# A new issue order for a fused attention and feed-forward kernel: five engine queues, copy engines and ring buffers

## The chip, the cores and the metric

The kernel runs on one core of one Trainium2 chip. The metric is device time in microseconds (us). The three runs of the kernel before took 398.63, 402.89 and 396.58 us; their median is 398.63.

A core has five engines with a queue of instructions each, which each works off in order: TensorE (PE in the profile, with its weight loads PEld), VectorE (DVE), ScalarE (ACT), GpSimd (POOL) and SyncE (SP, which here only issues DMAs). They wait for each other by semaphores.

## What is computed

Causal attention with a decay from forget gates, over 8 batches, 8 heads, 576 positions and head width 64; the heads are then joined and go through a bilinear feed-forward layer with 4608 tokens, width 512 and inner width 1536.

```python
scores = scale * np.matmul(q, k.transpose(0, 1, 3, 2))
cum = np.cumsum(np.log(np.clip(f, 0.0001, 1.0)), axis=-1)
decay = cum[:, :, :, None] - cum[:, :, None, :]
scores = np.where(causal, -1000000000.0, scores + decay)
attn = softmax(scores)                      # over the last axis
x = np.matmul(attn, v).transpose(0, 2, 1, 3).reshape(4608, 512)
out = ((x @ w_a) * (x @ w_b)) @ w_out
```

## The kernel before, in words

**Work items.** The function builds a list `ops` of 2353 numbered operations (class `Op`), each with an engine (or a choice of engines), a function that issues its instructions, and the operations on which it depends. Costs, priorities and due times that are noted at each operation came from a planner and play no part any more: the order in which the operations are issued is written out in the string `ORDER` (operation numbers, a range where they follow one another). Each engine executes its own operations in that order. The string `CHOICE` gives a letter (D, A or P for DVE, ACT or POOL) for each operation that several engines can do: casts, copies out of PSUM and, in batches 0 and 1, the normalisation of the attention weights. The string `SLOTS` gives, ring by ring, the buffer number of each tile in the order in which tiles are taken. `laid_out` (L1330) reads `ORDER` and `CHOICE`; `slot` and `turn` (L158, L161) read `SLOTS`.

**Attention.** The 64 heads are worked in 32 pairs `t`, four pairs to a batch. For each pair, PE computes scores for five blocks of 128 query rows, in three steps `qk t.0`, `qk t.2` and `qk t.3` (L529 to L605). For the pairs from 4 on, a fused DVE instruction adds the decay and finds the row minimum (L674); for batch 0 the decay is added by more matmuls, and DVE only finds the maximum (L646). ACT takes the exponential with its row sum (L701, L705), DVE the reciprocal (L713, L715), and POOL (in some cases of batches 0 and 1 ACT) normalises the weights (L726, L724) in two tiles, PA for query blocks 0 to 2 and PB for blocks 3 and 4. The weights are transposed: in batch 0, and for part A in batch 1, by PE (`ptr`, tile psP) with a copy out of PSUM (`pev`), everywhere else by a transposing DMA from SP (`tr`, L740) into PTA and PTB. PE then multiplies with v (`pv`, tiles pv and pvx, L769 and L784) and a copy (`ev`) puts the result into xT, which the feed-forward reads.

**Loads.** q, k and v of a batch come by DMA: q and k in two halves each (`ld`), f32 into a ring of three landing buffers n32 by SP, then cast to f16 by POOL (`ca`), transposed by PE (`pt`, tile psT) and copied to qT or kT (`pe`). Batch 0 and the v of batches 0 and 1 are cast by the DMA itself, which POOL issues (L334, L305). POOL also issues the eleven loads of the weights wa, wb and wout (L510). The cumulated decay rows come by DMA to the tile spread, 24 times, or are spread by PE (`bm`, tile scd) with a copy (`bc`) for pairs 4 to 7.

**Feed-forward.** It is cut into blocks of 256, 256, 256, 384, six times 512, and 384 tokens. For each slice of 128 to 256 of the inner width PE computes psa = x wa and psb = x wb; ACT copies psa to f16, and DVE multiplies it with psb into a tile ht (L1073). pso = h wout follows, with a copy (`ocopy`) and a store. psa, psb, pso, the transposes and the spread tiles share four PSUM buffers `ff`; scores and pvx share two double ones, `sc`.

**Interleaving.** Feed-forward blocks whose tokens are done are issued between the attention steps of later pairs. At the start, before any xT is there, PE is kept busy with 24 `wake` operations of four dummy matmuls (L82). The matmuls have modes: row (two tiles of 64 rows: scores and transposes of q and k), column (two tiles of 64 columns: pv) and full.

**Operations that are spoken of below.** 2: identity; 5 to 28: wakes; 46 and 47, 58: loads of k of batch 0 (first half in two parts, second half); 52 and 53, 62: the same of q; 48, 49, 54, 55, 59, 63: their transposes; 50: copy of the first k; 66 to 70: v loads of batch 0; 71 to 78: loads of wa, wa, wb, wb (first third of the width) and wa, wa, wb, wb (the rest); 82: scores 0.0; 262, 274, 267, 279: k and q loads of batch 1; 275, 280: casts of its second halves; 287: a fill of POOL; 500: first q load of batch 2; 1061, 1097, 1098, 1099: last scores, A and B transpose and pv of pair 19; 1465, 1501, 1503: the same (without B) of pair 27; from 1707 on: feed-forward.

Of the kernel before, what the change touches and what calls it, by code (L numbers as in the profile page):

```python
# [25 lines left out]
def kernel(  # L26
# [13 lines left out]
    B, H, S, D = q.shape  # L40
# [64 lines left out]
    def paddings():  # L105
# [36 lines left out]
        PA:03210213021302130213021302130213;PB:01101010101010101010101010101010;S:010110100110100110101011001101  # L142
        01010101001010101010101010010011010100101001000100010011011010011100111011010101110101;a16:0210210210210
        21021021021021021021201201210210210210201201201012012021021021020120120201010201210201201201201201021;bc
        :0210210210210210210210210210;ff:03120312032100023120310323231232301230103010103203013120312031203120312
        03123012310120213203203013203210312013201320130123021312312031232013012013023103210131310321320312031023
        10210321032130230231023102312302130213021321023023012032032031310210210312310231302132013203210310231023
        20120210102120321312012013203103021301321301302102302310230132031203120132013012012021023101301321032132
        030231031031032031230123201230312312312312312312302311021021302301231231230;ht:0dcba981234567d0bc9a18234
        5670dbc9a182543d670cb9a1428653d70cb2a9154863d7bac025914863dcb7a9205148dc36a9b72051483cdb6;n16:0110100101  # L150
        10001010010101010101;n32:0210201201201201020101212110210220201212202101;nv:01010101;osb:0101010101001010
        10101010010100110101;qd:010101010101010101010101;sc:0101010101010101010101011010010101100010101011001001
        0101101010101011010101010101010100101011101100101010110101100101100100101010;st:054321503421503421503421
        50342150
# [1054 lines left out]
    for n in cuts:  # L1209
# [3 lines left out]
        0 1 29 30 46 2 52 62 5 3 31 37 32 38 33-36 39 40 42 41 53 47 58 4 43 267 262 279 6-9 54 48 10 56  # L1213
# [27 lines left out]
        630 1792-1794 618 493 491 1795 492 494 631 702 707 653 654 703 697 1797 569 704 626 623 632 619  # L1241
# [4 lines left out]
        1827 1829-1831 709 719 723 767 671 681 591 729 628 724 647 636 682 655 648 641 1828 666 1832 686  # L1246
# [15 lines left out]
        1920 1914-1918 929 918 766 1919 951 970 975 1014 852 851 896 895 1871 919 1921 958 920 959 955  # L1262
# [111 lines left out]
```

## Time and profile before

| | |
|---|---|
| median of three runs | 398.63 us (396.58 to 402.89) |
| span of the profiled execution, from the first to the last instruction | 397.5 us (its own total time is not listed beside it) |
| PE busy | 386.4 us (97%), 5768 matmuls |
| DVE busy | 293.0 us (74%) |
| ACT busy | 290.6 us (73%) |
| POOL busy | 257.8 us (65%) |
| DMA | 76.87 MB, mean 193 GB/s |

A row of the timeline shows the start, the duration, the engine, the line, and the tiles written and read, with a count where instructions of one kind follow each other; in brackets stands the idle time ahead of it and what ended it. A row of the grouped view shows busy time, mean duration in ns, and idle time ahead by what ended it. A matmul's end is modelled and its 0.17 us or so of run-out overlaps the next one, so for PE the distance between starts says more than a duration. A row of the DMA issues shows kilobytes and the median time to landing.

### The profile page before, as it was taken

What the parts mean: (1) busy time and instruction counts of PE and PEld (TensorE: products, weight loads), DVE (VectorE), ACT (ScalarE), POOL (GpSimd) and SP (SyncE); (2) the same over time, 40 slices, a digit from 0 to 9 for tenths busy, and PEclk for the clock granted to TensorE, in tenths of its full rate; (3) what the DMA queues carried; (4) which work ended last, traced back from release to release, by engine and by line L of the source; (5) the groups of instructions that cost most, each with busy time, mean ns of one, the idle gap of its engine ahead of it and who ended that gap; (6) DMA issues with size and microseconds to landing.
All of it is one profiled execution on the core that took longest, in us unless ns stands there. A gap on an engine that the chain in (4) does not pass through costs nothing.

```text
span 397.5 us, 14691 instructions
## 1 busy us (share of the span) xinstructions
PE 386.4 (97%) x5768; PEld 250.9 (63%) x5768; DVE 293.0 (74%) x971; ACT 290.6 (73%) x805; POOL 257.8 (65%) x464
## 2 busy tenths in 40 slices
PE   6899999999999999999999999999999999999997
PEld 3557887969766665655555665555555556567785
DVE  7888798999998779787888798668878772333131
ACT  5999899999879778778988588898878763232131
POOL 8689687769887679884996877779936871000000
PEclk9999999999999999999999999999999999999999
DMA  7999999999999999999999999999999586100202
GB/s 117 256 195 167 157 147 226 220 285 283 244 188 228 238 293 234 235 249 292 231 205 278 223 255 214 248 258 206 252 220 230 104 147 156 63 2 1 81 28 81
DMA packets 147365, 76.87 MB, mean 193 GB/s; under 512 B 124384, under 2 KB 128352, under 8 KB 147296
## 3 DMA queue, kind: packets, MB, share of 16 engines
q1 hardware_dynamic: 132856, 68.72, 77.7%
q0 software_dynamic: 14256, 7.08, 14.7%
q8 instruction: 45, 0.74, 0.8%
q14 instruction: 24, 0.20, 0.2%
q10 hardware_dynamic: 184, 0.14, 0.1%
HBM read 52.05 MB, written 9.58 MB: 155 GB/s over the span
## 4 chain that ended last, share of the span: by engine, by line
PE 77%; DMA 11%; POOL 4%; ACT 3%; issue 2%; DVE 2%; SPq 0%; DVEq 0%; ACTq 0%; POOLq 0%
PE psa L74 21%; PE psb L74 20%; PE pso L74 20%; PE sc L551 4%; DMA PTA<-PA 3%; PE pvx L769 3%; POOL PA L726 2%; DMA PTB<-PB 2%; PE psT L359 2%; DMA wb<-in_moe_w_b_dram 2%; PE sc L539 2%; DMA wout<-in_q_dram 2%; PE sc L74 1%; PE psP L74 1%; DMA k<-in_k_dram 1%
## 5 line engine op out<-in xcount | busy, mean ns | idle before, releaser
L674 DVE CUSTOM_DVE_ANT_0 S<-sc,spread 64x576 f32<-64x576 f32 (+4 forms) x232 | 125.9, 562 | 17.3 <-ACT PA L705 8.3
L74 PE MATMUL psb<-xT,wb 128*64 128x512 f16 (+2 forms) x1056 | 113.9, 341 | 0.8 <-DMA wb<-in_moe_w_b_dram 0.5
L74 PE MATMUL psa<-xT,wa 128*64 128x512 f16 (+2 forms) x1056 | 114.1, 341 | 0.0
L289 ACT CAST a<-psa 128x512 f16<-128x512 f32 (+1 forms) x114 | 63.3, 559 | 56.4 <-PE psa L74 52.3
L1073 DVE TENSOR_TENSOR ht<-psb,a 128x512 f16<-128x512 f32 (+1 forms) x114 | 74.4, 658 | 38.5 <-PE psb L74 27.7
L74 PE MATMUL pso<-wout,ht 128*64 128x512 f16 x840 | 102.4, 380 | 0.0
L726 POOL TENSOR_SCALAR PA<-PA,st 128x256 f16<-128x256 f16 (+2 forms) x180 | 84.9, 483 | 8.8 <-DVE st L715 5.5
L705 ACT ACTIVATE PA<-S,st 128x256 f16<-128x256 f32 (+2 forms) x168 | 84.2, 504 | 6.5 <-DVE st L674 6.0
L74 PEld LDWEIGHTS <-wb 128*64 128x64 f16 x1056 | 62.5, 110 | 30.0 <-issue 2.5
L74 PEld LDWEIGHTS <-wa 128*64 128x64 f16 x1056 | 61.7, 110 | 29.3 <-issue 2.2
L726 POOL TENSOR_SCALAR PB<-PB,st 128x512 f16<-128x512 f16 (+1 forms) x90 | 63.4, 711 | 24.3 <-DVE st L715 10.7
L74 PEld LDWEIGHTS <-ht 128*64 128x64 f16 x912 | 49.9, 110 | 33.0 <-issue 1.9
L705 ACT ACTIVATE PB<-S,st 128x512 f16<-128x512 f32 x56 | 40.2, 720 | 3.3 <-DVE st L674 3.0
L705 ACT ACTIVATION_READ_ACCUMULATOR PA<-S,st 128x1 f32 x168 | 32.1, 191 | 0.0
L701 ACT ACTIVATE PB<-S,st 128x576 f16<-128x576 f32 x28 | 21.7, 775 | 9.8 <-POOL PA L726 3.1
L631 POOL TENSOR_SCALAR_AFFINE_SELECT spread<-spread 128x768 f32<-128x768 f32 x24 | 20.9, 870 | 10.1 <-DMA spread<-cum_d 10.0
L769 PEld LDWEIGHTS <-nv 128*64 128x64 f16 x640 | 21.7, 110 | 7.5 <-DMA PTA<-PA 2.1
L674 DVE CUSTOM_DVE_ANT_1 S<-sc,spread 128x256 f32<-128x256 f32 x48 | 19.8, 419 | 6.9 <-PE sc L539 2.0
L715 DVE RECIPROCAL st<-st 128x2 f32<-128x2 f32 x128 | 18.3, 156 | 6.9 <-ACT PB L705 3.5
L674 DVE DVE_READ_ACCUMULATOR2_ANT st<- 128x1 f32 (+1 forms) x280 | 23.0, 82 | 0.0
L551 PE MATMUL sc<-kT,qT 64*128 64x512 f16 (+4 forms) x144 | 20.8, 326 | 1.2 <-ACT kT L289 0.4
L289 ACT COPY osb<-pso 128x512 f32<-128x512 f32 x24 | 13.8, 580 | 9.1 <-PE pso L74 7.8
(106 smaller groups left out, 483.2 us busy)
## 6 DMA issues: line engine op xcount, KB each, us to landing
spread<-cum_d SPq DMA_DIRECT2D x24, 576.0 KB, 6.4
out_dram<-osb SPq DMA_DIRECT2D x35, 256.0 KB, 3.4
q<-in_q_dram SPq DMA_DIRECT2D x14, 576.0 KB, 5.7
k<-in_k_dram SPq DMA_DIRECT2D x14, 576.0 KB, 5.0
v<-in_v_dram SPq DMA_DIRECT2D x24, 256.0 KB, 6.0
wout<-in_moe_w_out_dram POOLq DMA_DIRECT2D x3, 512.0 KB, 7.5
nv<-in_v_dram POOLq DMA_DIRECT2D x8, 128.0 KB, 5.1
wa<-in_moe_w_a_dram POOLq DMA_DIRECT2D x2, 512.0 KB, 7.5
```

Of the source, the lines that this page charges most:

```text
L74: nc.tensor.matmul(out=out[r], lhsT=lhsT[:, r], rhs=rhs, **kw)
L289: nc.scalar.copy(out=out_, in_=in_)
L359: nc.tensor.matmul(out=p[m][HP[j] if quad else slice(0, 128), 64 * t:64 * t + 64], lhsT=x[r, j, t, :] if quad else x[r, t, :], rhs=ident16 ...
L551: nc.tensor.matmul(out=dst, lhsT=lhsT, rhs=rhs, start=start, stop=stop, skip_group_check=True)
L631: nc.gpsimd.affine_select(out=c[:, :, 0:SM].rearrange("p h (j k) -> p h j k", k=128), in_=c[:, :, SM:2 * SM].rearrange("p h (j k) -> p h j ...
L674: nc.vector.tensor_tensor_reduce(out=o, in0=x, in1=y, scale=-1.0, scalar=3e38, op0=ADD, op1=MIN, accum_out=m)
L701: nc.scalar.activation(out=p_blocks(t, 4), in_=T[("s" if direct else "z", t, 4)], func=EXP, bias=st[:, 8:9], scale=sign, accum_out=st[:, 1 ...
L705: nc.scalar.activation(out=p_blocks(t, i)[:, :, h, :], in_=(T[("s", t, i)][:, h, :] if direct else T[("z", t, i)][:, h * n:h * n + n]).rea ...
L715: nc.vector.reciprocal(out=st[:, 20 + 2 * i:22 + 2 * i], in_=st[:, 10 + 2 * i:12 + 2 * i])
L726: VEC[e].tensor_scalar(out=p, in0=p, scalar1=st[:, c:c + 1], scalar2=1.0, op0=MUL, op1=MUL)
L769: nc.tensor.matmul(out=o[HP[h], 128 * i:128 * i + 128], lhsT=vt[:, j, pr + NP * h, :], rhs=pt[:, base_blk[i] + 2 * block_at(t, i, j) + h, ...
L1073: nc.vector.tensor_tensor(out=ht[:, 0:n_], in0=T.pop(("psb", t0, fbs))[:, 0:n_], in1=T.pop(("a16", t0, fbs))[:, 0:n_], op=MUL)
```

## The change

Nothing but the three strings changes: `SLOTS`, `ORDER` and `CHOICE`. All 2353 operations stay, with their functions and tiles. In the new strings 9 more of the operations with a choice are DVE's, 12 fewer ACT's and 3 more POOL's. Of the copies of q and k out of PSUM 16 go from ACT to DVE and 11 the other way, of the output copies 11 and 6, of the normalisations 12 from ACT to POOL and 9 back. The dependences are the same; PE has the same 576 operations in another order. The first lines of each string:

```diff
     SLOTS = """
-        PA:03210213021302130213021302130213;PB:01101010101010101010101010101010;S:010110100110100110101011001101
+        PA:01230312031203120312031203120312;PB:01101010101010101010101010101010;S:01011010100110101010101110101
...
     ORDER = """
-        0 1 29 30 46 2 52 62 5 3 31 37 32 38 33-36 39 40 42 41 53 47 58 4 43 267 262 279 6-9 54 48 10 56
-        50 44 11 63 82 55 83 12 13 49 45 85 91 97 57 65 64 86 92 87 93 51 94 14 127 59 130 136 88 99 98
-        95 96 287 66 61 67 268 90 263 60 288 172 15 131 16 138 132 137 128 269 17 175 181 176 177 183
...
+        0 2 5-10 29 3 46 48 1 31 52 54 47 37 53 11 62 58 4 45 30 32 38 44 33-36 56 287 74 50 82 49 39 51 40 85
+        43 66 55 91 12 71 41 86 13 93 92 87 42 83 500 69 70 67 63 57 127 64 97-99 59 88 89 130 136 90 60 65 72
+        131 137 14 132 15 94-96 172 175 181 100 138-140 16 17 101 176 182 177 183 288 289 128 142-144 141 290
...
     CHOICE = """
-        DDDDADADADAAPPAPPPAPPAADAPPPPPPAPADDDDPPPAPPPPPDDDDPAAPAPPPADDDADAADAAAADDPPPAPAPPPADDAAPPAP
+        DDDDDAADDDADAPPPPPPAPDAADPPPPPPPPADDDDPPAPPPPPPDDDAAAPAAPPPPADDADDDAADAADAPPPAPAPAPADDAPPPPPAPPPADDAPPP
```

The order of SP around pair 19 reads, in the kernel before, 17A, 18A, two loads and a spread load, 19B, 19A, and after the change 17A, a spread load, 18A, a q load of batch 6, 19A, a q load, a spread load, 19B.

More of the change, by code (lines that the diff above doesn't have):

```diff
@@ L147 @@
[L147 to L151, printed above, removed]
@@ L152 @@
-        10101010010100110101;qd:010101010101010101010101;sc:0101010101010101010101011010010101100010101011001001
-        0101101010101011010101010101010100101011101100101010110101100101100100101010;st:054321503421503421503421
-        50342150
+        PA:01230312031203120312031203120312;PB:01101010101010101010101010101010;S:01011010100110101010101110101
+        010010111010101010110101010010110101010101001000101101101011010101101010100010110110101;a16:01201201201
+        2012012012012012012102102102101201201201201201201021021021021012012012010201021012012121010120120210210
@@ new lines @@
+        ;bc:0120120120120120120120120120;ff:0123012301203103211130130320101010321030030332310230231023102310231
+        0321031203103210320320123213013021032103213021302230213020323021312032103210320130123102123012301230121
+        3210321320132013213013013012301230123012302130213021301201230120320120320302131230123012032130213023023
+        1012010203202312310321032120312031201230123012301231210230231021320312013012310231023012310230202312301
+        3201231320320120132010321023013201312012013213213201320320120123120312031203120312;ht:0123456789abcd012
@@ L155 @@
+        3456789abcd0123456789ab01cd2345678901ab23cd4567018923ab45cd0167238945ab01cd2367458901ab23cd046715;n16:0
+        10101011110001010010110110101;n32:0121221102012010012010212101202120120102102011;nv:01010101;osb:010101
+        010101010101101101010000110101;qd:010101010101010101010101;sc:01010101010101011010101010010101011001011
+        010101010101010100101010101010101010101010110101010010101010101010010101001010101010101;st:012345012345
+        01234501234501243501
     """
@@ new lines @@
+        268 227 232 222 228 229 114 234 159 233 223 262 342 263 145 343 391 190 192 178 180 269 84 179 184 270
+        186 191 271 225 235 237 236 103 264 24 166 167 25-27 104 230 121 147 28 105 109 110 265 106 185 231 203
[4 rows of a table added]
+        238-240 1720 306 1718 244 245 1722 123 124 298 344 345 1724 273 197 81 347 349 355 354 356 170 246 241
[4 rows of a table added]
+        1741 496 1743 375 376 370 359 1742 377 369 445 371 398 1744 420 307 504 446 315 427 284 378 1745-1748
+        328 329 372 314 374 1749 1750 447 421 521 428 1751 330 331 1752 215 422 423 1753 216 424 448 449 337
@@ new lines @@
+        338 333 429 451 452 1754 403 459 426 465 353 453 454 458 460 507 379 334 430 419 411 467 360 461 1755
+        1757 455 1756 1759 1761 466 412 462 1758 450 1735 497 1760 472 473 373 1762-1764 335 384 498 499 468
[3 rows of a table added]
+        435 490 1772 1773 437 438 568 572 609 525 514 471 482 483 516 532 534 544-546 548 515 571 615 1775 573
+        1776 554 556 1777 719 555 557 439 440 702 703 579 1779 1781 1778 1780 1783 570 610 558 586 559 707 560
+        1769 574 581 587 1782 533 488 588 1785 1787 580 1784 1786 589 590 582 552 697 593 594 441 442 1789 1791
@@ new lines @@
+        1788 1790 541 575-577 1774 547 592 612 653 616 617 553 623 540 624 583 1793 493 585 494 1792 595 618
[3 rows of a table added]
+        668 644 646 1817 1819 1821 647 1816 723 662 670 1818 709 648 674-676 1822 1820 677 1823 708 663 720
[9 rows of a table added]
+        1880 1867 839 840 813 856 1868-1870 806 1881 911 792 834 829 858 862 793 815 912 841 864 863 844 865
+        870 866 869 871 872 845 925 1882 1884-1886 805 1883 1888-1890 876 878 868 877 873 836 879 1887 1892
[6 rows of a table added]
+        854 985 982 1101 951 1108-1110 1927 1924 986 897 1057 943 898 1930 997-999 945 1931 1111 1928 1929 1014
@@ new lines @@
+        964 971 973 1016 1020 1022 1027 1932 1021 1019 1028-1030 1940 1023 1034 1002 1003 1063 1941-1943 1036
[7 rows of a table added]
+        1091 1123 1124 1132 1155 1139 1976 1978 1152 1977 1979 1084 1980-1982 1303 1146 1121 1033 1983 1984
[4 rows of a table added]
+        1239 1098 1176 1189 1999-2001 1165 1166 1184 1306 1199 1200 1307 1309 1992 2003 1158 1159 1201 1099
[5 rows of a table added]
+        1241 1325 1246 2033 1234 2034-2036 1330 1263 1277 1332 1336 1289 1343 1344 2037-2039 1198 1338 1346
+        1345 2040 1247 1261 1279 1292 1293 1337 2042 2044 2041 1285 1294 1328 1295 1339 1334 2043 2045 1326
@@ new lines @@
+        1373 2046 1190 2048 2049 1183 1197 1256 1296-1298 1270 1271 1350 1352 2050 1351 1353 1340 2047 1357
+        1358 1331 1322 2051 1333 1324 1286 1362 1363 2052 2054 1323 2053 2055 1510 1511 1359 1364 1365 1278
+        1374 1376 1380 1394 1381 1272 1354 1211 1255 1356 2056 1417 1395 2057 2058 1360 1317 1382-1384 1290
+        1291 1388 1390 1299 1387 1397 1385 1379 1366 1367 1396 2059-2061 2007 1257 2062 2063 1319 1389 1258
+        1423 1378 1401 1402 2064 2066 2067 1375 1377 1512 1406 1407 1213 1513 2068 1514 1214 2069 1300 1318
@@ new lines @@
+        1418 2071 2065 1403 1398 1420 1409 1424 1408 1432 1431 1438 1439 1426 1434 1301 2072 2073 1404 1399
+        1361 1386 1433 1410 1461 1302 1462 1412 1425 1427-1429 1464 1440 1468 2074 1469 1441 1475 1442 1470
[7 rows of a table added]
+        2119 1619 1416 1549 2120 2122 1554 2121 1578 1523 1559-1561 1582 1533 1590 1535 1556 1437 1589 2124
[4 rows of a table added]
+        1627 1568 2141 1640 1635 2144 1642 2142 2145 1586 1641 2133 1557 1594 1606 1629 1630 2146-2148 2150
+        2149 2151 1643 1631 1569 1570 1530 1634 1636 1607 1666 1670 1614 1684 1671 1588 1677 2152 2154 1587
@@ new lines @@
+        2153 2156 1637 1678 1672 1680 1679 1681 1685 2158 1543 1572 1683 2157 1527 1616 1624 1673 1674 1632
+        1647 1686 2159-2161 1644 1645 1668 1648 1621 1649 2155 2162 1558 2164 1595 1646 2166 2165 2168 1544
+        2167 2163 1639 2170 1687 2169 1688 1690 2172-2174 2176 2177 1623 1691 1692 2175 1665 1693 1682 1689
+        1652 2171 1653 1667 1654 1602 2178-2182 1655 1656 2183 1571 1615 1696-1698 1528 2143 1573 1694 1638
+        1699 1700 2184 2186 2188-2190 2192 2193 1617 2185 1574 1650 1657 2187 2191 2194 2197-2199 2202-2205
@@ new lines @@
+        2195 1659 2207 1676 1618 1695 1675 1703 1701 1651 1658 1702 1660 1661 1704-1706 2196 1662 2200 2201
+        2208-2216 2218 2217 2219-2224 2226 2228 2229 2225 2230 2232 2234 2233 2227 2235 2236 2238 2237 2239
+        2231 2240 2242 2244 2241 2245-2250 2252-2254 2251 2255 2256 2258 2206 2243 2257 2259 2280 2282 2281
+        2283 2260 2284-2286 2288 2290 2287 2289 2261 2262 2265 2263 2266 2267 2270-2272 2275 2276 2268 2269
+        2264 2273 2274 2277 2278 2292 2294 2291 2293 2296 2298 2297 2300 2299 2295 2302 2301 2303 2304 2306
@@ L1323 @@
+        2305 2307 2308 2310 2312 2309 2279 2314 2316 2311 2318 2313 2315 2320 2322 2317 2319 2324 2326 2321
+        2323 2325 2328 2327 2329 2330 2333 2334 2331 2332 2335-2340 2343 2344 2341 2342 2345 2346 2348 2349
+        2347 2350-2352
     """
     CHOICE = """
-        DDDDADADADAAPPAPPPAPPAADAPPPPPPAPADDDDPPPAPPPPPDDDDPAAPAPPPADDDADAADAAAADDPPPAPAPPPADDAAPPAP
-        PAPAADADAAAPPPPPPDDDAPPPPPPPPPAADAAAAADADDAAAAADADDADADDAADDDAADAADDDADADDAAAADADDAADAAAADDA
-        AAAADADAAAADAAAADAAADAAAAADADAAAADAADDAADDDAAAD
+        DDDDDAADDDADAPPPPPPAPDAADPPPPPPPPADDDDAPPAPPPPPDDDAAAPAAPPPPADDADDDAADAADAPPPAPAPAPADDAPPPPPAPPPADDAPPP
@@ L1328 @@
+        PPPPAPDADDPPPAPPPPPADAAADADADDADAAAADADDAAADAAADDADDDDDADAADAAADAADAADADDAAADAADDAAADDAAADADADAAAAADADA
+        DDDAAAADADDADADDAADDAADDA
     """
```

20 lines of the change are left out of this document (1 added, 19 removed), and 148 rows, old and new, of the table ORDER.

## The prediction

> **What bounds the kernel now.** I read the page first (engine shares, and the sizes of the loads), then the waits of TensorE alone, then the busy time of every engine in a few stretches.
>
> ```profile
> span 397.5 us, 14691 instructions
> ...
> PE 386.4 (97%) x5768; PEld 250.9 (63%) x5768; DVE 293.0 (74%) x971; ACT 290.6 (73%) x805; POOL 257.8 (65%) x464
> ...
> q<-in_q_dram SPq DMA_DIRECT2D x14, 576.0 KB, 5.7
> ```
> ```profile
> PE pvx L769 <- DMA PTA<-PA: 1.3, 3, 0.8
> ...
> PE psb L74 <- DMA wb<-in_moe_w_b_dram: 0.5, 1, 0.5
> ```
> ```profile
> 2.78:35.63 32.85, 29.96 (x544) 17.68 (x544) 28.02 (x68) 27.71 (x83) 27.93 (x55) 1.00 1.06 201
> ```
> ```profile
> 35.63:393.83 358.20, 355.84 (x5214) 1.00 0.94 195
> ```
> ```profile
> 329.83 6.04 PE pso L74 x56
> ```
>
> The columns of the first stretch are its length, then the busy time of PE, weight loads, DVE, ACT and POOL, granted clock, DMA share and GB/s; the second has PE alone. The reader should see two kernels. From the first feed-forward matmul (35.63 us) to the last (393.83) TensorE is idle 358.20 - 355.84 = 2.36 us of 358. In the quiet end 28 pairs of matmuls follow each other in 6.04 us, 0.216 us a pair, so busy there means streaming. Before 35.63 us PE is filled with 24 dummy "wake" groups while the softmax of batch 0 runs on ACT, DVE and POOL, each busy 28 of 32.85 us. A new order removes no work from PE; it can only shorten the start, remove the 2.4 us, or lose them again and more.
>
> The Trainium skill (Perfetto Trace Analysis, Identifying the Most-Contended Engine) calls the matmul busy share a bad measure and would judge by the share of weight loads, here 63%, which leaves 37% of room, a time down to some 250 us. The row of 56 pso matmuls does not agree that this room is there.
>
> **The change, part by part.** Operations, tiles and the dependences between them are the same; what moves are positions in five queues, the engine of some copies, and buffer numbers. I compared the two printed lists operation by operation.
>
> *The start.*
>
> ```profile
> 2.78 4.00 PE L74 MATMUL wake<-ident 128*64 128x512 f16 x20 [2.78 <-POOL ident masks.py:199]
> ...
> 9.32 0.48 PE L359 MATMUL psT<-ident,wout 64*64 64x64 f16 x36 [0.83 <-DMA wout<-in_q_dram]
> 9.73 0.34 PE L551 MATMUL sc<-kT,qT 64*128 64x256 f16 x4
> ```
> ```profile
> 35.63 1.06 PE L74 MATMUL psa<-xT,wa 128*64 128x256 f16 x16
> 36.53 1.34 PE L74 MATMUL psP<-ident,PB 128*64 128x128 f16 x42
> ```
> ```profile
> 1.33 0.80 POOL L334 DMA_DIRECT2D k<-in_k_dram  x1 [0.81 <-POOLq L1358]
> ...
> 14.06 0.38 POOL L726 TENSOR_SCALAR PA<-PA,st 128x128 f16<-128x128 f16 x1 [2.92 <-DVE st L715]
> ...
> 14.54 1.83 POOL L305 DMA_DIRECT2D nv<-in_v_dram  x2
> ...
> 21.56 0.68 POOL L510 DMA_DIRECT2D wa<-in_moe_w_a_dram  x1
> ```
> ```profile
> 7.80 0.63 ACT L289 COPY kT<-psT 128x576 f16<-128x576 f16 x1
> ```
> ```profile
> L293 POOL CAST k<-k 128x1152 f16<-128x1152 f32 x14 | 16.0, 1143 | 2.2 <-DMA k<-in_k_dram 1.8 <-PE psT L359 0.3
> ...
> L289 ACT COPY kT<-psT 128x576 f16<-128x576 f16 x19 | 11.7, 638 | 2.3 <-PE psT L359 2.3
> ...
> L293 DVE COPY kT<-psT 128x576 f16<-128x576 f16 x13 | 9.8, 752 | 0.9 <-PE psT L359 0.5
> ...
> L289 ACT COPY xT<-psP 128x768 f16<-128x768 f16 x6 | 4.8, 801 | 0.1
> ...
> L724 ACT ACTIVATE PA<-PA,st 128x256 f16<-128x256 f16 x4 | 2.1, 522 | 0.0
> ...
> L289 ACT COPY spread<-scd 128x512 f32<-128x512 f32 x3 | 1.7, 574 | 0.2 <-PE scd L74 0.2
> ```
>
> POOL makes the identity before the first k load instead of after it: the wakes start up to 0.8 us sooner (the 0.80 of that issue), the k load leaves some 0.6 later, the q load behind it at the same time; no cost. The first scores (op 82) move ahead of the transposes that waited until 9.32 for a load: they can start when the copy of k, ending at 7.80 + 0.63 = 8.43 on ACT, is done, not at 9.73. That copy goes to DVE (0.75 for 0.64), ahead of the second half of the scan, which the scores of the larger blocks need; I credit 0.8 of the 1.3 us. From the first exponential to the last weight of pair 3 that the first feed-forward block needs, ACT loses three q/k copies (3 x 0.64), two copies of transposed weights (2 x 0.80), together 3.5; it gains one q/k copy (0.64), two spread copies (2 x 0.57) and two normalisations (2 x 0.52), together 2.8. Net -0.7, with the 0.8 above -1.5 at pair 3. Behind it PE now runs the four batch-0 transposes that stood behind the first psa (the 36.53 row and ten matmuls more, some 1.5 us), so the first psa itself stays near 35.6 while that work is already done. POOL is moved the other way at first: one wb, two wa and four v loads now stand ahead of its first norm, 3 x 0.68 + 4 x 0.92 = 5.7 us in a gap of 2.92, so that norm comes some 2.8 later; two v loads, three weight issues and two casts (1.14 each) leave the stretch behind it, 6.2 us, so by pair 3 POOL is 3.4 ahead. I take -1.2. Bounds: +1.0, if the later scan ends last (a copy of 0.75 and its hand-over), and -3.4, if POOL's queue ended last.
>
> *The second half of wb.*
>
> ```profile
> 37.07 8.06 DMA wb<-in_moe_w_b_dram
> ```
> Its last issue stands two norms earlier in POOL's queue, and both second-half casts of batch 1 come behind it. The 0.5 us that psb waited goes: -0.5, bounds -0.5 and 0. The late casts (q and k) have their transposes at the same PE position as before; the two ops are hidden by the attention of batch 1, and cost at most their 2.3 us if POOL falls behind.
>
> *Loads.* On SP the first q load of batch 2 now stands ahead of all four loads of batch 1 and holds one of the three landing buffers until its cast, far behind the first psa. Batch 1's two second halves then wait for a cast each, and everything behind them on SP with them. The transposes of batch 1's first q move from behind PE's 12th wake to behind its 19th, some 7 wakes or 3 us, so this is covered; without the cover it costs the 576 KB ahead, about 2.9 us at the 201 GB/s of the stretch row above. Cost 0.
>
> *Engines.* Nine copies net go from ACT to DVE and three norms from ACT to POOL: DVE +6.8 us (9 x 0.752), ACT some -7, POOL +2. DVE is busy 74% of the span and PE waited for a copy or a product in none of the long waits: hidden, cost 0, and 6.8 if DVE were the one that PE waits for.
>
> *Changes between row-tiled and full matmuls.*
>
> ```profile
> 154.03 0.86 PE psb L74 x8
> 155.48 0.98 PE psa L74 x8
> ```
> A group of eight takes 0.12 us longer when it follows score or transpose matmuls. Counted in the two lists, the steps into and out of them fall by five (full to row 51 to 59, row to full 59 to 53, column to row 12 to 5): -0.6, bounds -0.6 and 0.
>
> *Attention weights that PE waits for.* The chain is score matmul, decay, exponential, norm, transposing DMA, weighted sum (pvx); PE takes its queue in order, so a late one stops the feed-forward behind it.
>
> ```profile
> 197.09 0.38 PE L551 MATMUL sc<-kT,qT 64*128 64x512 f16 x2
> ```
> ```profile
> 212.50 1.57 SPq L740 DMA_TRANSPOSE PTB<-PB  x1
> 214.13 2.80 SPq L740 DMA_TRANSPOSE PTA<-PA  x1
> ```
> ```profile
> 222.07 0.33 PE L769 MATMUL pvx<-PTA,nv 128*64 128x128 f16 x6
> ```
> ```profile
> DMA to landing us min/median/max: 3.7/5.6/6.7
> ```
> ```profile
> 280.01 0.39 PE L551 MATMUL sc<-kT,qT 64*128 64x512 f16 x2
> ```
> ```profile
> 295.52 1.90 SPq L740 DMA_TRANSPOSE PTA<-PA  x1
> ```
> ```profile
> 301.75 0.36 PE L769 MATMUL pvx<-PTA,nv 128*64 128x128 f16 x6
> ```
>
> Pair 19: last score at 197.09, A transpose issued at 214.13 and landed by the median 5.6 later, 22.6 us after the score; pvx came at 25.0. Between these two PE operations stand 23 groups of eight before and 16 after: 7 x 0.863 (6.04 us over seven groups) = 6.0 us less, so 19.0. That is a wait of 3.6 us if the chain keeps its length.
>
> ```profile
> 192.31 0.39 PE L551 MATMUL sc<-kT,qT 64*128 64x512 f16 x2
> ```
> ```profile
> 203.19 3.29 SPq L740 DMA_TRANSPOSE PTA<-PA  x2
> ```
> The neighbour, pair 18, whose A is the second of this row, was through 16.5 to 19.8 us after its score. On SP pair 19's A now goes ahead of its B, but B comes behind two loads. Between a chain like pair 18's (no wait) and its own (3.6) I take the middle, 1.8. Pair 27: chain 21.1, pvx at 21.7, two groups and one pvx (0.7) less, 19.3: 0 to 1.8, I take 0.9. The three waits of now (1.3) stay but for one whose distance grows by half a microsecond: -0.4. Sum +2.3, bounds -1.3 (all waits go) and +5.4 (both pairs at full length). By the same count no other pair's distance falls more than half a microsecond below its chain.
>
> **Sum.** -1.2 - 0.5 + 0 + 0 - 0.6 + 2.3 = 0.0 us on the profiled 397.5: what the start gains, two late pairs take. Its own total time is not given beside the span; the median of the three runs, 398.63 (396.58 to 402.89), lies 1.1 above the span. So 398.6 us. From the bounds: -5.8 (-3.4 - 0.5 - 0.6 - 1.3) to +6.4 (+1.0 + 5.4), 392.8 to 405.0.
>
> **The rivals.**
>
> *Slower: one late pair stops PE.* In before the longest chain of a pair is that of pair 12:
>
> ```profile
> 126.68 0.38 PE L551 MATMUL sc<-kT,qT 64*128 64x512 f16 x2
> ```
> ```profile
> 153.39 3.75 SPq L740 DMA_TRANSPOSE PTA<-PA  x2
> ```
> 153.39 + 5.6 - 126.68 = 32.3 us, where the list left 37. If pair 19 gets such a chain in its 19.0 us, PE waits 13.3 instead of 1.8: about 410. For it: the SP queue is in order, and a load that waits for a buffer stands right ahead of pair 19's A transpose. Against: pairs 18, 19 and 27 took 17 to 23 us. It decides from 8 us over the forecast, a chain of 29.
>
> The Trainium skill (TensorE: Matmul & The Clock Gate, Part 1) says that PE falls back to half clock after about 3.4 us without work and needs as long to return. The first wakes bear it out in their durations, not in the granted clock, 1.00 in the stretch row: ten pairs take 4.00 us, where 0.216 each makes 2.2. A long wait would cost such 1.8 us once more, 412 instead of 410.
>
> *Faster: the start shrinks to PE's own work.*
>
> ```profile
> L74 PE MATMUL wake<-ident 128*64 128x512 f16 x96 | 15.0, 425 | 2.8 <-POOL ident masks.py:199 2.8
> ```
> The 48 pairs of wakes would take 10.4 us instead of 15.0, and 2.9 us of idle time would go: 7.5, with 0.5, 0.6 and 1.3 from the later parts 9.9, so 388.7. Against it: ACT, DVE and POOL are busy 85% of that stretch and keep nearly all their work.
>
> *The start's gain holds.* Pairs 19 and 27 come in time, as pair 18 did, and their 1.8 and 0.9 go: 398.6 - 2.7 = 395.9. The rows of pair 18 speak for it, those of pairs 19 and 27 themselves against.
>
> **How the numbers follow.** Forecast 0.39 and "the gain holds" 0.26 both end within 2% (390.7 to 406.6, about what a measurement of this kernel can tell from no change): 0.65. The late pair 0.26, the short start 0.09. The likeliest's own range is 392.8 to 405.0. The range given reaches towards both other cases, up to the slow rival's 410 and down to half the way to 388.7: 391.5 to 410.
>
> **What would show it.** In the changed profile: the first psa between 34 and 37 us with batch-0 transposes of PB ahead of it; psb without a wait for wb; a PE wait for a transpose ahead of pair 19's pvx, near 220 us, of 0 to 4 us; PE idle between first psa and the end between 1 and 8 us. Wrong would be a wait of PE of many microseconds on a load or a transpose elsewhere, or a first psa before 33 us.

## The result, and the profile after

The changed kernel takes 413.19 us (median of four, 409.22 to 413.86) against 398.73 (median of four) of the kernel before, in the same job: a ratio of 1.0341, 95% interval 1.027 to 1.0412. It is slower by 14.5 us; the forecast of 398.6 and its range up to 410.0 are both missed. Here and below a median is of all four runs, while a ratio leaves out a run that took over 1.5% longer than its kernel's fastest, so the two can differ a little.

The page of the changed kernel's profiled execution:

```profile
span 412.1 us, 14675 instructions
...
PE 393.1 (95%) x5768; PEld 255.5 (62%) x5768; DVE 297.7 (72%) x980; ACT 285.2 (69%) x793; POOL 258.8 (63%) x467
...
PEclk9989999889999999999999999999999999999999
```

PE is busy 393.1 us instead of 386.4 with the same 5768 matmuls: some of them ran slower. The row of the granted clock, in slices of 10.3 us, has an 8 at 21 to 31 us and two at 72 to 93, where before had 9s throughout. The waits of PE in the changed kernel (in all, times, longest):

```profile
PE pv L784 <- DMA nv<-in_v_dram: 4.0, 1, 4.0
PE pvx L769 <- DMA PTA<-PA: 3.1, 4, 1.6
PE pv L769 <- DMA nv<-in_v_dram: 1.8, 1, 1.8
```

Of these three, before had only the one for PTA (1.3); PE waited for no load of v. The wait for wb (0.5) is gone. Two stretches of the changed kernel (columns as in the prediction), then the same two of before:

```profile
20.00:34.00 14.00, 12.04 (x184) 6.98 (x180) 9.09 (x23) 10.38 (x32) 9.56 (x17) 0.88 1.48 214
...
80.00:90.00 10.00, 9.75 (x154) 8.19 (x156) 6.31 (x26) 5.55 (x17) 6.89 (x10) 0.70 0.30 88
```
```profile
20.00:34.00 14.00, 13.12 (x230) 8.31 (x228) 11.75 (x28) 13.43 (x39) 12.84 (x25) 1.00 1.00 189
...
80.00:90.00 10.00, 10.00 (x199) 6.39 (x196) 9.71 (x38) 9.38 (x27) 6.58 (x13) 1.00 1.18 289
```

The third number from the right is the granted clock: 0.88 and 0.70 where before had 1.00. The first stretch has the first wait for v in it, the second begins at the end of the other. Within them the trace of the changed kernel has a granted clock of 0.50 from 27.99 to 31.41 and from 79.19 to 86.02 us, and 1.00 ahead of and behind each. Here is PE around the second wait, then around the first:

```profile
75.97 0.25 PE L784 MATMUL pv<-PTB,nv 128*64 128x64 f16 x4
80.25 0.37 PE L784 MATMUL pv<-PTB,nv 128*64 128x64 f16 x6 [4.03 <-DMA nv<-in_v_dram]
80.43 0.51 PE L769 MATMUL pv<-xT,nv 128*64 128x128 f16 x6
80.73 1.92 PE L74 MATMUL psb<-xT,wb 128*64 128x256 f16 x16
82.44 1.91 PE L74 MATMUL psa<-xT,wa 128*64 128x256 f16 x16
```
```profile
25.21 0.62 PE L74 MATMUL wake<-ident 128*64 128x512 f16 x4
25.67 0.28 PE L769 MATMUL pv<-xT,nv 128*64 128x128 f16 x4
27.73 0.25 PE L769 MATMUL pv<-xT,nv 128*64 128x128 f16 x2 [1.79 <-DMA nv<-in_v_dram]
27.82 2.85 PE L74 MATMUL wake<-ident 128*64 128x512 f16 x12
30.41 0.58 PE L769 MATMUL pv<-xT,nv 128*64 128x128 f16 x6
```

Read the starts. A psb or psa of 16 matmuls takes 0.87 us at full clock; behind the wait the next starts after 1.71, and so do two more: 3 x 0.84 = 2.5 us on top of 4.0. Ahead of the first wait a wake (four matmuls) takes 0.46 us from start to start; behind it three take 2.59 (27.82 to 30.41), 0.86 each, which adds 1.2.

Where do these loads come from? POOL's queue, in the changed kernel and then in before:

```profile
55.94 0.73 POOL L305 DMA_DIRECT2D nv<-in_v_dram  x1
...
63.19 0.20 POOL L621 MEMSET spread<- 128x128 f32 x1 [4.42 <-DVE st L674]
...
66.88 0.53 POOL L611 COPY qd<-qT 64x64 f16<-64x64 f16 x2 [1.65 <-ACT qT L289]
...
69.94 0.93 POOL L305 DMA_DIRECT2D nv<-in_v_dram  x1
```
```profile
54.76 3.37 POOL L305 DMA_DIRECT2D nv<-in_v_dram  x4
```

Operation 284, a 128 KB load of v for batch 1, is one of the four in a row of before, at 55.48 us, 17.0 us ahead of pv4 of pair 4 (72.48), which needs it. In the changed kernel it stands 14 us behind its neighbour at 55.94: ahead of it are two waits of POOL (4.42 for a spread buffer, 1.65 for a copy of q), six norms, three casts and the two small operations that wait. It is issued 6.0 us ahead of the same pv4 (75.97). The chain that ended last has both loads in it (start, duration):

```profile
14.26 13.43 DMA nv<-in_v_dram
...
69.94 10.27 DMA nv<-in_v_dram
```

They are operations 67 (batch 0) and 284, and take 13.43 and 10.27 us from issue to landing. For all ten loads of nv, in the changed kernel and in before:

```profile
DMA to landing us min/median/max: 3.5/9.8/13.4
```
```profile
DMA to landing us min/median/max: 3.8/5.1/7.2
```

So the two waits are not quite of one kind. The first load has lost no lead: it is issued 11.4 us ahead of the first weighted sum (14.26 to 25.67), where before had 11.2 (15.48 to 26.65); it lands later. The second has lost 11 of its 17 us and lands late as well: had it landed in the 7.2 us that no load of v exceeded in before, the 6.0 us of lead would have left a wait of at most 1.2 us instead of 4.0 (an estimate from these rows).

To see where the 14.6 us between the spans arise I use PE's lag: the start of an operation less the sum of the slots of all operations ahead of it in PE's queue. A slot is the distance to the next start, for each kind its 10% quantile in the trace of before (0.87 for the psa above). The sum is 367.6 us for both orders, so lags can be compared at the same operation:

| PE's lag, us | first psa (1707) | psa 1753 | pso 1767 | psb 1827 | pso 1993 | last psz |
|---|---|---|---|---|---|---|
| before | 10.8 | 12.4 | 12.9 | 14.8 | 21.9 | 26.5 |
| after | 13.1 | 15.7 | 23.3 | 27.1 | 35.4 | 41.3 |
| 284 up (second run below) | 11.0 | 14.4 | 15.8 | 19.6 | 27.6 | 33.5 |
| both v up (third) | 10.3 | 15.1 | 16.8 | 20.6 | 30.5 | 37.1 |
| fill (fifth) | 13.4 | 14.6 | 20.7 | 26.3 | 36.1 | 41.3 |
| before, 284 late (sixth) | 9.7 | 10.9 | 18.3 | 20.2 | 25.9 | 30.5 |
| 284 up, pv later (last) | 10.7 | 12.6 | 14.0 | 17.6 | 25.7 | 33.0 |

After against before, from left to right: +2.3 at the first psa, +1.0 to 1753, **+7.1** to 1767 (the wait of 4.0, the clock behind it 2.5), +1.9 to 1827 (pair 8), +1.2 to 1993, +1.3 to the end.

### The profile page after: what moved, and what is told of

Read it like the earlier page. It is cut to its first block, busy times and chain, and to the rows that moved or that the text cites. A ratio compares the mean times of both kernels' runs of the same rounds, so it can differ in the third digit from the quotient of the medians.

```text
span 412.1 us, 14675 instructions
## 1 busy us (share of the span) xinstructions
PE 393.1 (95%) x5768; PEld 255.5 (62%) x5768; DVE 297.7 (72%) x980; ACT 285.2 (69%) x793; POOL 258.8 (63%) x467
## 3 DMA queue, kind: packets, MB, share of 16 engines
q0 software_dynamic: 14256, 7.08, 13.9%
## 4 chain that ended last, share of the span: by engine, by line
PE 67%; DMA 17%; POOL 7%; DVE 4%; issue 4%; ACT 1%; POOLq 0%; DVEq 0%; ACTq 0%
PE psa L74 18%; PE psb L74 18%; PE pso L74 16%; DMA PTA<-PA 6%; DMA nv<-in_v_dram 6%; PE pvx L769 3%; PE sc L551 2%; DMA out_dram<-osb 2%; PE sc L539 2%; DMA spread<-cum_d 2%; DVE S L674 1%; PE psT L359 1%; PE sc L74 1%; DMA PTB<-PB 1%; POOL PA L726 1%
## 5 line engine op out<-in xcount | busy, mean ns | idle before, releaser
L674 DVE CUSTOM_DVE_ANT_0 S<-sc,spread 64x576 f32<-64x576 f32 (+4 forms) x232 | 124.5, 562 | 14.6 <-ACT xT L289 2.6
L74 PE MATMUL psb<-xT,wb 128*64 128x512 f16 (+2 forms) x1056 | 116.3, 345 | 2.0 <-issue 1.2
L1073 DVE TENSOR_TENSOR ht<-psb,a 128x512 f16<-128x512 f32 (+1 forms) x114 | 74.1, 658 | 36.3 <-PE psb L74 26.3
L74 PE MATMUL pso<-wout,ht 128*64 128x512 f16 x840 | 99.6, 380 | 0.2 <-DVE qT L293 0.2
L705 ACT ACTIVATE PA<-S,st 128x256 f16<-128x256 f32 (+2 forms) x168 | 83.9, 502 | 13.4 <-DVE st L674 13.2
L726 POOL TENSOR_SCALAR PB<-PB,st 128x512 f16<-128x512 f16 (+1 forms) x92 | 65.0, 712 | 40.9 <-DVE st L715 17.0
L726 POOL TENSOR_SCALAR PA<-PA,st 128x384 f16<-128x384 f16 (+2 forms) x181 | 84.9, 480 | 8.9 <-DVE st L715 5.7
L74 PEld LDWEIGHTS <-wb 128*64 128x64 f16 x1056 | 64.6, 112 | 32.2 <-issue 4.9
L74 PEld LDWEIGHTS <-wa 128*64 128x64 f16 x1056 | 63.1, 111 | 28.6 <-issue 2.0
L289 ACT COPY osb<-pso 128x512 f32<-128x512 f32 x19 | 11.1, 582 | 23.5 <-PE pso L74 19.6
L715 DVE RECIPROCAL st<-st 128x2 f32<-128x2 f32 x128 | 18.3, 156 | 9.1 <-ACT PA L705 6.4
L674 DVE CUSTOM_DVE_ANT_1 S<-sc,spread 128x256 f32<-128x256 f32 x48 | 19.6, 419 | 6.3 <-ACT PB L705 2.0
L293 DVE COPY osb<-pso 128x512 f32<-128x512 f32 x16 | 11.0, 685 | 17.4 <-PE pso L74 13.9
L638 POOL TENSOR_SCALAR_AFFINE_SELECT spread<-spread 128x256 f32<-128x256 f32 x24 | 9.8, 407 | 21.2 <-DVE st L674 21.2
```

Source lines behind the costliest of these rows:

```text
L74: nc.tensor.matmul(out=out[r], lhsT=lhsT[:, r], rhs=rhs, **kw)
L289: nc.scalar.copy(out=out_, in_=in_)
L293: VEC[e].tensor_copy(out=out_, in_=in_)
L638: nc.gpsimd.affine_select(out=x, in_=x, compare_op=mybir.AluOpType.is_ge, fill=NEGBIG, base=0, pattern=[[0, 2], [-1, 128]], channel_multip ...
L674: nc.vector.tensor_tensor_reduce(out=o, in0=x, in1=y, scale=-1.0, scalar=3e38, op0=ADD, op1=MIN, accum_out=m)
L705: nc.scalar.activation(out=p_blocks(t, i)[:, :, h, :], in_=(T[("s", t, i)][:, h, :] if direct else T[("z", t, i)][:, h * n:h * n + n]).rea ...
```

## The experiments

The theory was: a late load of v stops PE twice, and PE's clock falls behind each stop. Rivals: another resource is late next; the batch loads on SP crowd the v loads; the engines cost the time. Unless the text says otherwise a run is the changed kernel with operations moved in their queue by three lines in `laid_out`:

```diff
             o.eng = names[next(letters)] if len(o.durs) > 1 else next(iter(o.durs))
+        for n, m in ((66, 287), (67, 66),):
+            seq.remove(ops[n])
+            seq.insert(seq.index(ops[m]) + 1, ops[n])
         assert len(seq) == len(ops)
```

This is the first run; for the others only the pairs (operation, the one behind which it goes) are given. Times are medians of four, ratios stand to before in the same job.

**First v loads ahead of wb**: pairs (66, 287), (67, 66).

> The changed kernel with two loads of v of batch 0 (operations 66 and 67) moved ahead of the first load of wb on POOL's queue, where before had no weight load ahead of them. Theory (a late load of v stops PE, and the clock falls behind it): the 1.8 us that pv waits for a load of nv near 26 us goes, and with it the granted clock of 0.88 between 20 and 34 us; 4.3 us of the 14.6 go, 413.2 becomes about 409, first psa near 35 us. Rival (the batch-2 load on SP crowds the loads, not POOL's queue): the load still lands some 13 us after its issue and the time stays within 1 us of 413. Rival (the chain of pair 3 sets the first psa, the wait is covered): the wait goes, the first psa stays near 39.

410.16 us (406.75 to 412.98), 1.0259 (1.0188 to 1.033). The wait near 26 us is gone, and the first psa comes at lag 10.4 instead of 13.1. But psa and psb now wait 0.6 us each for a load of wa and one of wb. The operations that wait start at 42.15 and 45.29 us; in the changed kernel PE came to the same two at 44.16 and 46.84. So PE, which now comes earlier, meets loads that the first wait had hidden. The wait of 3.5 us for operation 284 stays, and the one for pair 18's transpose grows from 0.25 to 2.3 in this execution. By the medians 3.0 us are won, by the ratios 3.3, where 4.3 were expected, and the intervals overlap.

**One load of batch 1 up**: pair (284, 286).

> The changed kernel with one load of v of batch 1 (operation 284) moved up POOL's queue, from behind norm4.0 (69.9 us) to behind its neighbour 286 (56 us). Theory: the 4.0 us that pv4 of pair 4 waits for it at 76 us goes, and with it the clock of 0.70 between 80 and 90 us: 7.1 us of 14.6, 413.2 becomes about 406. Rival (something else is late next: tr4B, issued at 68.2 us behind two loads of v on SP): the wait moves to a transpose, and 2 us or less are won, 411 or more.

406.42 us (403.83 to 410.23), 1.0167 (1.0092 to 1.0242): 6.8 us for one DMA issue moved by 14 us, as the theory had it. Its waits of PE, and the stretch that had the clock of 0.70:

```profile
PE pvx L769 <- DMA PTA<-PA: 2.9, 3, 1.6
PE psT L359 <- POOL q L291: 1.5, 1, 1.5
...
PE pv L769 <- DMA nv<-in_v_dram: 0.5, 1, 0.5
```
```profile
80.00:90.00 10.00, 10.00 (x217) 6.98 (x215) 9.09 (x31) 9.13 (x25) 7.05 (x14) 1.00 0.87 179
```

The 4.0 are gone and the clock is full. The tr4B of the rival did not stop PE. The first wait, whose code is untouched, is 0.5 here, not 1.8: it varies from execution to execution (0.2 to 2.2 in the runs that share this start).

**Both**: pairs (66, 287), (67, 66), (284, 286).

> Both moves together. Theory: the gains add, 4.3 + 7.1 = 11.4, so about 402, 0.5 to 1% over before, with pv8's wait of 1.6 us and a diffuse 2.5 us between 160 and 270 us left. Rival (what the two waits hide comes out behind them): 405 or more.

408.85 us (407.45 to 409.61), 1.0251 (1.0206 to 1.0296). The gains do not add; the rival is right. Both waits for v are gone, and others are there:

```profile
PE pvx L769 <- DMA PTA<-PA: 4.5, 4, 2.0
PE psa L74 <- DMA wa<-in_moe_w_a_dram: 1.8, 1, 1.8
```

The psa that waits 1.8 us for wa starts at 43.30, still ahead of the 44.16 at which PE reached it in the changed kernel: the wait for v had hidden this load. Pair 18's transpose costs 2.0 in this execution, and behind that wait the granted clock is 0.50 from 221.2 to 224.6 us.

**SP's batch-2 load back**: pair (500, 279), with the buffers of n32 to match.

```diff
-n32:0121221102012010012010212101202120120102102011
+n32:1201210021201202202201102020121012012021021200
```

> The changed kernel with the first q load of batch 2 (operation 500) put back behind the four loads of batch 1 on SP, and its landing buffer to match; POOL's queue is untouched. Theory (POOL's queue makes the v loads late): both waits for nv stay, 412 to 414. Rival (the crowd of batch loads on SP at 9.4 to 11.3 us does): still three of these loads go out at once, but the loads of batch 1 land sooner; the first wait shrinks by more than half and 2 to 4 us go, 409 to 411.

412.59 us (410.72 to 414.28), 1.0348 (1.0291 to 1.0405), as the theory had it. The waits for v (the lines are 12 lower in this file):

```profile
PE pv L772 <- DMA nv<-in_v_dram: 3.9, 1, 3.9
...
PE pv L757 <- DMA nv<-in_v_dram: 0.3, 1, 0.3
```

The long wait stays, and so does the slow landing (operation 284 takes 10.11 us). That the short one is 0.3 tells nothing, since it varies by itself. The step that I had discussed at length, the q load of batch 2 on SP, is not where the time went.

**Fill**: the wait is kept, and PE kept at work in it.

```diff
-        for j in range(NSB):
+        for j in [0] * (70 if t == 4 else 0) + list(range(NSB)):
```

> The changed kernel; in pv4 of pair 4 alone the first matmul pair, whose operands are there, is issued 70 times more (3.6 us at the 0.051 us of a pair in pv4's row), so that TensorE works while the load of v is awaited. Nothing is left out. Theory (the clock falls because TensorE stands still): the load lands as late as before, the idle stretch of 4 us shrinks under 1 us, the granted clock between 80 and 90 us reads 1.00 instead of 0.70, and the time falls by about 2.5 us in spite of 140 more matmuls: about 410.5. Rival (the clock falls for another reason): still 0.70 there, 413.

415.51 us (413.91 to 417.76), 1.0412 (1.0331 to 1.0493). The clock did what the theory says:

```profile
80.00:90.00 10.00, 9.41 (x180) 7.30 (x178) 8.64 (x33) 8.08 (x23) 7.70 (x12) 1.00 0.36 66
```

1.00 instead of 0.70, and the lag from 1753 to 1767 grows by 6.1 instead of 7.6. The time did not fall. PE comes to pair 8's weighted sum 2.4 us earlier (117.94 instead of 120.31). There the gain goes: PE waits 1.89 instead of 1.62 us for the transpose, and this time the clock falls behind it, to 0.50 from 118.4 to 121.8 us; the lag grows by 5.6 to psb 1827, after 3.8 in the run without the fill. To 1993 it grows by 9.8 instead of 8.3: pair 18 waits 2.0 instead of 0.25 us, for weights that are no earlier (225.75, 225.10 without the fill). The fill also left 2.2 us of idle time, in its middle and put down to issue, not to the load. The part on the time is missed.

**Before, with that one load late**: the kernel before, pair (284, 527).

> The kernel before with only the load of v of batch 1 (operation 284) moved down POOL's queue, from 55.5 us to behind operation qd8 (70.5 us). Theory: issued at 70.6 us and landed 5 to 10 us later, it stops pv4 of pair 4, which came at 72.5, for 3 to 8 us, and the clock falls behind it by some 2.5 us more: 402 to 409, while TensorE's queue is untouched. Rival (a single load is not what costs, the whole order of the loads is): under 2 us, 400 or less.

404.86 us (403.13 to 406.63), 1.0127 (1.0052 to 1.0202), within the theory's 402 to 409: 6.3 us by the medians, 5.1 by the ratio. PE in this run:

```profile
70.92 0.25 PE L784 MATMUL pv<-PTB,nv 128*64 128x64 f16 x4
75.36 0.38 PE L784 MATMUL pv<-PTB,nv 128*64 128x64 f16 x6 [4.18 <-DMA nv<-in_v_dram]
75.54 1.90 PE L74 MATMUL psb<-xT,wb 128*64 128x256 f16 x16
```

The same picture, a wait of 4.18 and a psb of 1.69 us from start to start, made in the kernel before by moving one operation. From 1753 to 1767 the lag grows by 7.4 instead of 0.5; 1.4 of this are won back by the end. So the largest single loss of the change hangs on this operation's place in POOL's queue: it goes when the place is undone, and comes when the place alone is changed. The two cases are not the same in their parts: here the load is issued only 2.1 us ahead of pv4 (68.80 to 70.92) and lands in 6.52, in the changed kernel it is issued 6.0 ahead and takes 10.27. Why loads of v land late in the changed order is open; the fourth run shows only that the q load of batch 2 is not the reason.

**The new engines in the old order**: the kernel before with the new `CHOICE`.

> The kernel before in its own order, with the changed kernel's choice of engines (nine copies net from ACT to DVE, three norms from ACT to POOL). The prediction's term: 0, 398 (bounds 0 to 6.8). Rival (the loss that is left when the two waits for v are taken out, 7 us in the run with operation 284 moved up, comes from the engines): 402 to 405.

417.14 us (416.32 to 418.06), 1.0435 (1.0369 to 1.05). Neither case had 19 us. No load of v is among the waits (the one for a q load near the start, 0.8 in before, is 1.1); there are many small ones:

```profile
PE sc L551 <- DVE kT L293: 1.8, 1, 1.8
PE psP L74 <- ACT PA L724: 1.3, 2, 0.7
PE psa L74 <- ACT kT L289: 1.2, 1, 1.2
PE pv L784 <- DVE xT L293: 1.2, 1, 1.2
PE psa L74 <- DVE spread L293: 1.2, 1, 1.2
```

Copies and norms now stand in queues that were ordered for other engines; that this makes the waits is argued, not shown.

**The new order with the old engines**: the changed kernel with the `CHOICE` of before.

> The changed kernel's order and buffers with the engines of before. If the engines cost nothing: 411 to 414, with both waits for nv in the profile. If they cost the rest: 406 to 408. A third case: nine copies stand in queues that were not ordered for them, a new wait appears on ACT, and it is slower than 414.

426.67 us (425.73 to 427.38), 1.0671 (1.0605 to 1.0737): the third case. A wait of 4.2 us for nv is in it, and 13.5 us more than in the changed kernel, again in small waits. Order and engines belong together; neither has a price of its own.

**Casts into POOL's idle stretch**: pairs (284, 286), (67, 66), (280, 107), (275, 280). The second run left 1.5 us of waiting for a cast of q (280), which I took to be late behind two norms and a load; POOL is idle from 30.6 to 35.2 us in the changed kernel.

> The changed kernel with operation 284 moved up as in the second experiment, the load of v 67 directly behind 66 (ahead of the first wa load, not of wb), and the two late casts of batch 1 (280, 275) moved on POOL into its idle stretch between norm0.3 and norm0.4 (30.6 to 35.2 us). Theory (what is left at 40 us is POOL's queue: the transposes pt1q1 wait 1.5 us for a cast behind two norms and a load): that wait goes, 406.4 becomes about 405. Rival (the loads of batch 2 that follow these casts on SP go out some 8 us sooner and take the place of wa and wb, as a wa load was late by 1.8 us when both loads of v went first): a wait for wa or wb takes its place, 406 or more.

411.88 us (411.39 to 412.81), 1.0327 (1.0281 to 1.0372), 5.5 slower than the second run, and by neither of the two ways. POOL, then PE:

```profile
29.64 0.70 POOL L726 TENSOR_SCALAR PB<-PB,st 128x512 f16<-128x512 f16 x1
36.08 1.15 POOL L291 TENSOR_SCALAR q<-q 128x1152 f16<-128x1152 f32 x1 [5.75 <-DMA q<-in_q_dram]
```
```profile
40.45 0.25 PE L74 MATMUL psP<-ident,PB 128*64 128x128 f16 x2 [4.82 <-POOL PB L726]
```

The q load is not there yet. The trace of the second run had said so: there POOL stands 3.81 us right ahead of this cast (start 41.05), for the load and not for the norms. Here POOL waits 5.75 us for it with a norm behind the cast, and PE stands 4.82 us for that norm. My own move made the fault that the change had made: it filled an idle stretch of an in-order queue without asking when the operand lands.

**Weighted sums later**: the previous kernel, and (563, 1813), (564, 563), (809, 1918), (810, 809), (1055, 1993), (1056, 1055).

> The previous kernel, and on TensorE the weighted sums of pairs 8, 13 and 18 one or two feed-forward groups later, each with its copy (behind operations 1813, 1918 and 1993). Theory (the attention weights of these pairs have no slack in the changed order): the waits for PTA, 2.9 us in the run with 284 alone, fall to about 1 us as in before (1.3), so another 1.5 to 2 us: about 403. Rival (the whole of ACT, DVE and POOL is late there, and the next pair waits instead): the waits for PTA stay near 3 us, time as in the previous kernel.

411.38 us (410.84 to 412.72), 1.0321 (1.0264 to 1.0379): no different from the previous kernel; waits for PTA 2.3 instead of 3.6 us.

**The same without the casts**: (284, 286) and the six pairs of the run above.

> The changed kernel with operation 284 moved up, and the three weighted sums later, without the casts. Theory: 406.4 - 1.5 to 2 = about 404.5, waits for PTA about 1 us. Rival (the next pair waits instead): 406, waits near 3.

404.46 us (403.34 to 405.56), 1.0138 (1.0089 to 1.0186): the theory's number, but not by its way.

```profile
PE pvx L769 <- DMA PTA<-PA: 2.6, 3, 1.1
PE wake L74 <- POOL ident masks.py:199: 1.4, 1, 1.4
PE sc L539 <- ACT kT L289: 1.3, 1, 1.3
```

The waits for PTA are 2.6, not 1, and from 1753 on its lag grows by 20.4 us against 19.1 in the second run. Its lead is there by 1753 (12.6 against 14.4), where the wait for the cast of q happens not to occur, and the moved sums had not yet come. So the moves of pv won nothing that can be shown. This version has the lowest median of the changed order, though its interval overlaps that of the second run; none beats the kernel before.

## Why the prediction was wrong, point by point

**What bounds the kernel** was right: PE without idle time, and a new order that can "lose them again and more". The prediction even named the sign: "a wait of PE of many microseconds on a load". It gave it no term.

***Loads*, the step that failed.** "Cost 0" was worked out for SP's queue alone: the q load of batch 2, the two second halves behind it. The loads of v are issued on POOL, and of these the prediction counted the four at the start, as 0.92 us of POOL's time each in front of a norm. It never asked when they land and which matmul waits for them, and it did not look at operation 284 at all. The trace of before and the two lists held the question: four issues in a row, operation 284 among them 17 us ahead of its use, and a new list in which norms, casts and a fill that waits for DVE stand between 286 and 284. In place of the 0 the runs put the second load at 6.8 us (moved back in the changed kernel) and 5.1 to 6.3 (moved late in before), the first at about 3 with an overlapping interval. The other part that the term lacked is the landing: 9.8 us in the median instead of 5.1, which no run explains. The SP step that was discussed is worth 0.6 of 413.2, which is not measurable.

***The start*: -1.2 forecast, +2.3 measured at the first psa.** It came at 39.39 us, not between 34 and 37. Up to the first wait the forecast was even too small: at the last scores of pair 0 (operation 84) PE's lag is 7.5 us against 9.6 in before, 2.1 ahead. The wait of 1.8 for the first v load and the slow wakes behind it (1.2, and a fourth) take this back. With at most 0.5 us of that wait the first psa comes at lag 10.3 to 11.0, against 10.8 in before and 9.7 in the run of before with 284 late, whose start is the same: the gain of the start is not larger than what two executions of one start differ by. What takes the 2.1 us between operation 84 and the first psa when there is no wait was not separated.

***The second half of wb*: -0.5, right.** The wait is gone. The sentence on "both second-half casts", at most 2.3 us if POOL falls behind, has its size in one run (1.5), but there the cast waited for its own load and not for POOL.

***Engines*: 0.** DVE did not become the bound, but the step is not separable: the engines alone cost 18.6 us, the order alone 28.1, both together 14.5. A sum in which moved work and moved places are separate terms cannot say this.

***Mode changes*: -0.6, not borne out.** The count left out the steps from row to column, which rise from 4 to 9. With them the steps into and out of the row mode are 130 in both lists. The price was also read at the wrong place: from start to start the psb of the quoted pair, ahead of the transposes, takes 0.99 us (153.84 to 154.83), and the psa behind the scores 0.89 (155.41 to 156.30). In the trace of before from 95 us on the median of such a group of eight is 0.97 ahead of scores or transposes, 0.89 behind them and 0.86 between full ones. The dear step, full to row, rises from 51 to 59, which by itself is a small loss and not a gain. What the steps around pv cost was not separated.

***Attention weights*: +2.3 forecast on pairs 19 and 27.** Measured are waits of 3.1 instead of 1.3, so +1.8: nearly the size, by luck, for it came at other places. They are these:

```profile
120.31 0.36 PE L769 MATMUL pvx<-PTA,nv 128*64 128x128 f16 x6 [1.62 <-DMA PTA<-PA]
```
```profile
178.96 0.36 PE L769 MATMUL pvx<-PTA,nv 128*64 128x128 f16 x6 [1.06 <-DMA PTA<-PA]
206.95 0.36 PE L769 MATMUL pvx<-PTA,nv 128*64 128x128 f16 x6 [0.20 <-DMA PTA<-PA]
225.10 0.36 PE L769 MATMUL pvx<-PTA,nv 128*64 128x128 f16 x6 [0.25 <-DMA PTA<-PA]
```

These are pairs 8, 13, 16 and 18. Pair 19, pvx at 234.8, did not wait. I had taken the length of the chain from before and changed only PE's distance; but the chains changed too. Pair 8's last norm ends 13.0 us behind its last scores instead of 10.5, and that of pair 19's first three blocks 8.3 instead of 14.1.

**The rivals.** The slower one had the side, the size (410) and the clock right, and the wrong wait: pair 19's transpose for a load of v. Its price of a slow clock, 1.8 us by the first wakes, came out at 2.5 behind the second wait. The lower end of the range is a slip: half the way to 388.7 is 393.7 from the forecast, or 390.8 from 392.8, and not 391.5; nothing hangs on it.

**What stays open.** With operation 284 back and no wait left over 1.4 us the changed order is still 1.4% (0.9 to 1.9) slower. This rest lies in many pieces over the whole span (last row of the lags against before: +0.2 us up to 1753, +0.9 to 1767, +1.7 to 1827, +1.0 to 1993, +2.7 to the end); no run attributes them. Why the longest landing of a load of v is 12.4 to 13.9 us in the four runs that share the changed start, and so the first wait 0.2 to 2.2, is not settled either. The changed kernel's times spread from 409 to 414 together with the clock: the execution of 409.22 has a mean granted clock of 0.996, the others (412.57 to 413.86) 0.988 to 0.992. A stretch of 3.41 us at half clock is 0.004 of the mean, so these are one stretch against two or three. Which wait is shorter in the execution of 409.22 is not on record.

## What to carry to other kernels

When an order is replaced, list every DMA issue with its distance to the first reader, in the old order and in the new, on every queue that issues: a load that loses its lead is the first suspect, and one such load was worth nearly half of this loss. A lead that was long enough in the old order need not be in the new one, since the time to landing changes too. In an in-order queue a place is as late as the worst wait ahead of it, so an idle stretch may be filled only with work whose operands are there by then. And where PE is full, price a stop as the stop plus the slow clock behind it, but do not expect either back in full: the next chain without slack takes part of it.

## What the runs showed of the hardware that was not expected

Where the traces of these runs record the granted clock, it is either 1.00 or 0.50, and each stretch at 0.50 between the first and the last matmul is 3.41 or 6.83 us long. In the changed kernel one stands behind the wait of 1.79 us (27.99 to 31.41) and a double one at the wait of 4.03 (79.19 to 86.02). The length of the wait alone does not decide: behind waits of 3.5 and 3.9 us (first and fourth run) the stretch is a single one, and of two idle stretches of 2.2 us in the fill run the first was followed by one and the second by none. The Trainium skill (TensorE: Matmul & The Clock Gate, Part 1) says that PE falls back after about 3.4 us without work, seen in a window that runs freely. The lengths agree with such a window, and so does the distance between the two stretches of the changed kernel, 47.79 us or 14 x 3.41; that a wait of 1.79 us is enough does not agree with the 3.4 us without work.

Ten loads of v on POOL's queue, of 128 or 64 KB, landed 3.5 to 13.4 us after their issue in one execution of the changed kernel (3.8 to 7.2 in before).
